# A fused attention and two-MLP kernel: GpSimd's small steps moved or dropped, plain chunks first in block two, zero-padded low halves of k

## Chip, cores and metric

The kernel runs on one core of one Trainium2 chip. The metric is the device time of one execution in microseconds; three runs of the kernel before took 1105.09, 1108.4 and 1123.04 us, median 1108.4 us.

## The reference

Causal attention over 4 batches, 8 heads, 576 tokens and 64 features with a bias from a running sum, then two blocks. Block one adds the real part of a two-dimensional FFT to its input, normalizes, and adds an MLP (512 to 2048 to 512, ReLU). Block two is the same MLP step with a gain and no FFT. The MLP weights come in double precision.

```python
scores = q @ k.T / 8                       # per batch and head
cum = cumsum(max(s, 0))
scores += min(-(cum[:, None] - cum[None, :]), 0)      # causal: -1e9 above the diagonal
scores -= max(scores); attn = exp(scores)
x = attn / (sum(attn) + 1e-9) @ v
u = x + real(fft(fft(x, axis=1), axis=2))
un = (u - mean(u)) / sqrt(var(u) + 1e-6)
x = u + max(un @ w_ch1, 0) @ w_ch2         # block one
xn = (x - mean(x)) / sqrt(var(x) + 1e-6) * g_ln
out = x + max(xn @ w2_ch1, 0) @ w2_ch2     # block two
```

## The kernel before

**Tiles.** The 576 tokens of a batch are five row tiles: A0 and A1 (tokens 1 to 256), B1 and B0 (320 to 575, kept in reversed order), and M (token 0 and 257 to 319, 64 rows, two batches share 128). A unit is one pair of heads' row tile and head; a tile sees 129, 257, 320, 448 or 576 keys. Four pairs of heads per batch make 40 units.

**Two kinds of attention.** Batches zero and one (`attn_steps32`) multiply q and k in f32; the bias of batch zero is built on TensorE out of bf16 parts of the running sum (L1033 for the key's, L1036 for the query's, L1048 for the mask), that of batch one on GpSimd. Batches two and three (`attn_steps`) split q and k into fp16 high and low halves. `prep_pair` (L647) writes them into `qk16` and one transposing DMA (L692) turns them: block 0 and 1 hold a head's q as high and low halves below each other, 2 and 3 the high half of k twice, block 4 the low half of k, head 0 in rows 0 to 63 and head 1 in rows 64 to 127. `emit_qk` (L747) takes both heads of a tile together: for each a product of 128 rows (L757), then for each one of 64 rows with k's low half (L760), then the reduction on VectorE (L762). `turn_pair` (L699) copies the reversed and the M columns of q into `qx`, partly on GpSimd.

**A unit's way.** `emit_bias` (L731, GpSimd: an addition at L735, then a triangular mask at L740), `emit_qk` or `emit_qk32`, two exponentials on ScalarE (L785, L786), the low half of the probabilities by a subtraction (L796, GpSimd or VectorE), a transposing DMA, and the product with v (`emit_pv`, L830, L843). GpSimd also clears the padding of each probability tile (L784) and adds 1e-9 to the row sums (L810).

**MLP.** The rows go in chunks of two row tiles: `emit_ln` (L316) normalizes one. VectorE takes mean and variance and a power-of-two scale p; `un` (L343, a buffer of its own) and `u16` (high and low fp16 halves) follow, a transposing DMA makes `unT` (L351), and 14 operations of one or two columns (L354 to L365, GpSimd but for L357) make the correction `f` by three Newton steps; f is multiplied into the result at the end. Block one runs `emit_g1` (L377) and `emit_g2` (L401), with the next batch's attention and FFT put between them by `Side`. Block two runs `emit_g1x` (L443) and `emit_g2x` (L471), a product scheme with seven multiplications for eight: ReLU on ScalarE (L450), four sums on GpSimd (L451 to L454), a cast on ScalarE (L456), a subtraction on VectorE (L457). Its weights are prepared by `Weights7.split` (L289), whose sums (L295) are GpSimd's too.

**Block two's chunks.** `chunk2` (L1231) loads a chunk's rows from the scratch `x2d` into eight rotating slots of `xset`: A and M tiles by the SP queue (L1242), B tiles, whose rows are reversed, by an indirect gather that GpSimd issues (L1238). L1434 sets the order.

**Order.** Every engine executes its instructions in the order in which a list scheduler put them when the kernel was built; `urgent` raises priorities and `tc.issue_after` ties the issue of some steps to others. All plain DMAs are issued by the SP queue.

**Scratch.** `fwide` and `hwide` (L66, L70) lend the attention's rotating buffers of tiles B0 and B1 to the FFT: `ftile` are score tiles, `htile` with 0 probabilities and with 1 transposed probabilities.

## Time and profile before

| | |
|---|---|
| runs | 1105.09, 1108.4, 1123.04 us; median 1108.4 |
| profiled execution | 1109.54 us, span 1107.8 us |
| busy: TensorE, VectorE, ScalarE, GpSimd | 991.9, 723.0, 567.5, 616.1 us |
| granted TensorE clock, mean | 0.952 |
| HBM read, written | 61.50 MB, 9.51 MB |

The profile is of one execution. PE is TensorE's matmul, PEld its weight load, DVE VectorE, ACT ScalarE, POOL GpSimd, SP the queue that issues DMAs. In a timeline a row may stand for several instructions of one kind (xN): its first number is the start of the first, its second the time to the end of the last. A matmul's end is modelled, so successive matmuls overlap in it; how long one holds the array is read from one start to the next. An engine's wait is put down to what ended last before it.

### The profile page before, as it was taken

How to read it: one execution, taken by the hardware profiler on the slowest of the kernel's cores; microseconds unless marked ns; L12 is line 12 of the kernel's file. 1: busy time of each engine (PE TensorE's matmuls, PEld its weight loads, DVE VectorE, ACT ScalarE, POOL GpSimd, SP SyncE). 2: the span in 40 equal slices, each digit the busy share in tenths (PEclk: the TensorE clock that was granted, in tenths of full speed). 3: DMA queues.
4: the chain of work that ended last, by engine and by line, in shares of the span. 5: the costliest groups of instructions: out<-in, count | busy, mean ns of one | idle time of the engine just before them, and what ended most of it. 6: DMA issues, size and time to landing. Idle time of an engine off the chain costs nothing.

```text
span 1107.8 us, 23630 instructions
## 1 busy us (share of the span) xinstructions
PE 991.9 (90%) x8729; PEld 745.6 (67%) x8729; DVE 723.0 (65%) x1733; ACT 567.5 (51%) x1278; POOL 616.1 (56%) x1317
## 2 busy tenths in 40 slices
...
GB/s 197 258 193 247 234 139 139 140 137 113 124 135 197 181 161 2 66 183 159 179 43 147 54 248 286 19 49 39 57 22 39 58 21 50 47 39 21 20 10 30
DMA packets 286035, 124.19 MB, mean 112 GB/s; under 512 B 267616, under 2 KB 267872, under 8 KB 285920
## 3 DMA queue, kind: packets, MB, share of 16 engines
...
q14 instruction: 47, 0.39, 0.1%
HBM read 61.50 MB, written 9.51 MB: 64 GB/s over the span
## 4 chain that ended last, share of the span: by engine, by line
PE 40%; DVE 6%; POOL 4%; DMA 2%; issue 1%; ACT 0%; SPq 0%; POOLq 0%; DVEq 0%; ACTq 0%
PE acc L471 13%; PE g L443 7%; PE g1x L443 7%; PE g L401 6%; PE g L377 5%; DMA wbbig<-in_moe_w_ch_dram 1%; POOL wbsums L295 1%; DVE wbbig L156 1%; DVE wbbig L153 1%; DVE wb L156 1%; DVE wb L153 1%; PE pv L830 1%; DVE wbbig L150 0%; PE y L1153 0%; DVE h L384 0%
## 5 line engine op out<-in xcount | busy, mean ns | idle before, releaser
L377 PE MATMUL g<-unT,wa 128*128 128x256 f16 (+1 forms) x1920 | 221.6, 267 | 3.8 <-DMA unT<-u 2.6
L401 PE MATMUL g<-wa,h 128*128 128x512 f16 x864 | 211.9, 384 | 6.0 <-DVE h L384 3.4
L377 PEld LDWEIGHTS <-wa 128*128 128x128 f16 x1920 | 173.5, 100 | 45.2 <-issue 5.9
L471 PE MATMUL acc<-wbbig,wa 128*128 128x256 f16 x1512 | 181.6, 275 | 10.7 <-ACT wa L456 6.9
L457 DVE TENSOR_TENSOR wa<-wa,wa 128x896 f16<-128x896 f32 x72 | 81.1, 1126 | 161.2 <-ACT wa L456 161.0
L443 PEld LDWEIGHTS <-wb 128*128 128x128 f16 x1728 | 169.1, 98 | 20.3
L471 PEld LDWEIGHTS <-wa 128*128 128x128 f16 x1512 | 148.7, 99 | 31.4 <-ACT wa L456 7.4
L401 PEld LDWEIGHTS <-h 128*128 128x128 f16 x864 | 81.8, 99 | 87.8 <-DVE h L384 7.4
L456 ACT CAST wa<-wa 128x896 f16<-128x896 f32 x72 | 67.4, 938 | 129.8 <-POOL wa L454 129.8
L785 ACT ACTIVATE p<-sc,mn 128x576 f16<-128x576 f32 (+4 forms) x160 | 89.7, 576 | 64.6 <-DVE mn L762 21.8
L796 POOL TENSOR_TENSOR p<-sc,p 128x129 f16<-128x129 f32 (+4 forms) x104 | 92.1, 888 | 43.1 <-ACT sc L786 38.0
L453 POOL TENSOR_TENSOR wa<-wa 128x128 f32<-128x128 f32 x72 | 48.8, 678 | 102.8 <-ACT wa L450 102.6
L443 PE MATMUL g1x<-unT,wb 128*128 128x256 f16 x864 | 101.8, 273 | 0.0
L443 PE MATMUL g<-unT,wb 128*128 128x256 f16 x864 | 100.9, 273 | 0.0
L830 PE MATMUL pv<-v,pT 128*128 128x64 f16 x1632 | 69.4, 199 | 32.1 <-DMA pT<-p 12.2
L830 PEld LDWEIGHTS <-pT 128*128 128x128 f16 x1632 | 63.6, 102 | 47.0 <-issue 24.6
L786 ACT ACTIVATE sc<-sc,mn 128x576 f32<-128x576 f32 (+4 forms) x160 | 91.7, 574 | 1.4
L735 POOL TENSOR_TENSOR sc<-cumb,ncqs 128x320 f32<-128x320 f32 (+4 forms) x80 | 68.0, 860 | 21.6 <-DVE cumb L645 11.0
L383 ACT ACTIVATE h<-g 128x512 f16<-128x512 f32 (+1 forms) x80 | 43.5, 544 | 68.9 <-PE g L377 68.4
L784 POOL MEMSET p<- 128x128 f16 (+1 forms) x160 | 36.4, 248 | 75.5 <-DMA pT<-p 43.0
L1043 PE MATMUL s<-qkT 128*128 128x288 f32 (+4 forms) x192 | 69.8, 460 | 4.7 <-DVE total L84 2.2
L384 DVE SCALAR_TENSOR_TENSOR h<-g,h 128x512 f16<-128x512 f32 (+1 forms) x80 | 50.2, 628 | 30.0 <-ACT h L383 29.8
...
## 6 DMA issues: line engine op xcount, KB each, us to landing
...
```

The costliest lines, as they stand in the source:

```text
L377: nc.tensor.matmul(out=ps[:, c * i:c * i + c], lhsT=ch.w.w1(lw, kk, m + i), rhs=ch.unT[:, 4 * lx + kk, 0:c], start=(n == 0), stop=(n == 23),)
L401: nc.tensor.matmul(out=ch.ps[j], lhsT=h[:, lh, c:c + 128], rhs=ch.w.w2(lw, m + i), start=(m + i + n == 0), stop=(m + i == MB - 1 and n == 2),)
L443: nc.tensor.matmul(out=ps, lhsT=ch.w.w1(lw, kk, m + 8 * half), rhs=ch.unT[:, 4 * lx + kk, :], start=(n == 0), stop=(n == 11),)
L456: nc.scalar.copy(out=h[:, 0], in_=r[:, 0:7])
L457: nc.vector.tensor_tensor(out=h[:, 1], in0=r[:, 0:7], in1=h[:, 0], op=ALU.subtract)
L471: nc.tensor.matmul(out=acc[key], lhsT=h[:, lh, ia], rhs=b[:, ib, lw], start=(m == 0 and i == 0 and not second), stop=(m == 7 and i == 2 an ...
L735: nc.gpsimd.tensor_tensor(out=u.f[:, 0:n], in0=P.cumb[u.h][:, 0:n], in1=P.ncq[:, t, u.h:u.h + 1].to_broadcast([128, n]), op=ALU.add)
L785: nc.scalar.activation(out=u.w[:, 0:n], in_=u.f[:, 0:n], func=AF.Exp, bias=mn, scale=-1.0)
L786: nc.scalar.activation(out=u.f[:, 0:n], in_=u.f[:, 0:n], func=AF.Exp, bias=mn, scale=-1.0, accum_out=u.rs[:, h:h + 1])
L796: eng.tensor_tensor(out=u.w[:, w:w + n], in0=u.f[:, 0:n], in1=u.w[:, 0:n], op=ALU.subtract)
L830: nc.tensor.matmul(out=ps[:, c], lhsT=pT[:, lp * nb + kb, :], rhs=P.v[:, kb, lv, c], start=(n == 0), stop=(n == 3 * nb - 1),)
L1043: nc.tensor.matmul(out=ps[:, b - a:e - a], lhsT=P.qT[:, o:o + 128], rhs=kt[:, b - k0:e - k0], start=not pe, stop=not pe or (not masked and ...
```

## The change

- **Bias.** `emit_bias` loses its addition (L735): the running sum's value at the query's own position, constant in a row, drops out of the softmax. The mask reads the key's sums directly and over the full width. The sums are taken relative to their middle value. On TensorE the query's part (L1036) goes, and with it the tables that fed it and the transposes at the start (L605).
- **Correction of the normalization.** p is now a first estimate of the reciprocal root, and f a polynomial of the fifth degree on VectorE; the multiplication by `c2` moves to VectorE too. GpSimd has no part in it.
- **Small steps.** The 1e-9 goes to ScalarE (`tiny`); the probability tiles of A0, A1 and M are cleared once and stay; `turn_pair` needs only its VectorE copy, since q is loaded in the order of the row tiles (`load_q`).
- **Scores.** `qk16` gets a sixth block: k's low half of head 0 and of head 1 stand in blocks of their own whose other 64 rows are zero, so the second product uses all 128 rows. Heads are no longer taken two at a time. The transposing DMA moves 30 blocks in place of 25.
- **Buffers.** `un` takes turns with the FFT's scratch during block one; that scratch is now the score and transposed-probability buffers of tile B0.
- **Block two.** Three chunks of A tiles and the M chunk come first.

```diff
     def fwide(name):
         turn["f"] += 1
-        return ftile(name, (B1, B0)[turn["f"] % 2], turn["f"] // 2 % 2)
+        if turn["f"] % 2:
+            return ftile(name, B0, turn["f"] // 2 % 2)
+        return htile(name, B0, turn["f"] // 2 % 2, 1).bitcast(F32)
...
-            un = mpool.tile([128, 512], F32, tag="un", name="un", bufs=1)
+            un = un_tile[0]()[:, 0:512]
...
-        nc.gpsimd.tensor_tensor(out=v, in0=va, in1=p, op=ALU.mult)
-        nc.gpsimd.tensor_tensor(out=v, in0=v, in1=p, op=ALU.mult)
...
-        for _ in range(3):
-            t = va
-            nc.gpsimd.tensor_tensor(out=t, in0=v, in1=y, op=ALU.mult)
-            nc.gpsimd.tensor_tensor(out=t, in0=t, in1=y, op=ALU.mult)
-            nc.gpsimd.tensor_scalar(out=t, in0=t, scalar1=-0.5, scalar2=1.5, op0=ALU.mult, op1=ALU.add)
-            nc.gpsimd.tensor_tensor(out=y, in0=y, in1=t, op=ALU.mult)
-        ch.f = y
+        nc.vector.tensor_tensor(out=d, in0=p, in1=p, op=ALU.mult)
+        nc.vector.tensor_tensor(out=d, in0=d, in1=va, op=ALU.mult)
+        nc.vector.tensor_scalar(out=d, in0=d, scalar1=1.0, scalar2=None, op0=ALU.subtract)
+        f = small.tile([128, 2], F32, tag="f", name="f", bufs=3)[:, 0:n]
+        nc.vector.tensor_scalar(out=f, in0=d, scalar1=RSQRT[0], scalar2=None, op0=ALU.mult)
+        for c in RSQRT[1:]:
+            nc.vector.scalar_tensor_tensor(out=f, in0=f, scalar=c, in1=d, op0=ALU.add, op1=ALU.mult)
+        ch.f = f
...
-    qk16 = att.tile([128, 5, 5, 128], F16, name="qk16")
+    qk16 = att.tile([128, 6, 5, 128], F16, name="qk16")
...
             nc.vector.scalar_tensor_tensor(
-                out=qk16[:, 4, :, 64 * h:64 * h + 64], in0=raw[:, 1, :, h, :], scalar=sc[:, 1:2],
+                out=qk16[:, 4 + h, :, 64 * h:64 * h + 64], in0=raw[:, 1, :, h, :], scalar=sc[:, 1:2],
...
-        nc.gpsimd.tensor_tensor(
-            out=u.f[:, 0:n], in0=P.cumb[u.h][:, 0:n], in1=P.ncq[:, t, u.h:u.h + 1].to_broadcast([128, n]), op=ALU.add
-        )
...
         nc.gpsimd.affine_select(
-            out=u.f[:, a:n], in_=u.f[:, a:n], pattern=[[-1, n - a]], compare_op=ALU.is_ge, fill=MASKED, base=base,
+            out=u.f[:, 0:n], in_=P.cumb[u.h][:, 0:n], pattern=[[-1, n]], compare_op=ALU.is_ge, fill=MASKED, base=base,
...
-            pss = [ps_s.tile([128, 512], F32, tag="s", name="s")[:, 0:z - a] for _ in us]
-            for u, ps, qT in zip(us, pss, qTs):
+            for u, mn, qT in zip(us, mns, qTs):
+                ps = ps_s.tile([128, 512], F32, tag="s", name="s")[:, 0:z - a]
                 nc.tensor.matmul(out=ps, lhsT=qT, rhs=kT[:, 2 + u.h, a:z], start=True, stop=False)
-            for u, ps, qT in zip(us, pss, qTs):
-                r = slice(64 * u.h, 64 * u.h + 64)
-                nc.tensor.matmul(out=ps, lhsT=qT[r], rhs=kT[r, 4, a:z], start=False, stop=True)
-            for u, ps, mn in zip(us, pss, mns):
+                nc.tensor.matmul(out=ps, lhsT=qT, rhs=kT[:, 4 + u.h, a:z], start=False, stop=True)
...
-        if u.h == 1:
-            nc.gpsimd.tensor_scalar(out=u.rs, in0=u.rs, scalar1=1e-9, scalar2=None, op0=ALU.add)
+        if h == 1:
+            nc.scalar.activation(out=u.rs, in_=u.rs, func=AF.Identity, bias=tiny, scale=1.0)
...
-        chunks = [chunk2(wb, kk) for kk in KEYS[:7] + KEYS[8:] + KEYS[7:8]]
+        chunks = [chunk2(wb, kk) for kk in KEYS[0:5:2] + KEYS[8:] + KEYS[1:6:2] + KEYS[6:8]]
```

What the new order of instructions looks like at three places follows. The first is TensorE in the scores of batches two and three. Before, with L757 for the full products and L760 for those of 64 rows:

```order
L830 MATMUL pv<-v_4534,pT 128x64
L757 LDWEIGHTS qx
L757 MATMUL s<-qkT_104,qx 128x288
L757 LDWEIGHTS qkT_104
L757 MATMUL s<-qkT_104 128x257
L760 LDWEIGHTS qkT_104
L760 MATMUL s<-qkT_104 128x257
L760 LDWEIGHTS qx
L760 MATMUL s<-qkT_104,qx 128x288
L830 LDWEIGHTS pT
```

Now, with L756 for the high and L757 for the padded low half:

```order
L756 LDWEIGHTS qx
L756 MATMUL s<-qkT_105,qx 128x288
L757 LDWEIGHTS qx
L757 MATMUL s<-qkT_105,qx 128x288
L756 LDWEIGHTS qx
L756 MATMUL s<-qkT_105,qx 128x448
L757 LDWEIGHTS qx
L757 MATMUL s<-qkT_105,qx 128x448
```

High and low products of one unit now follow each other; two units are no longer woven into each other.

The second place is GpSimd where block two begins. Before: L295 are sums for the weights, L453, L451, L452 and L454 the sums of the hidden rows (`wa_188` and `wa_187` are the two scratch buffers), L354 and L355 steps of the normalization's correction, L1238 the gathers:

```order
L295 TENSOR_TENSOR wbsums<-wbbig 128x256 x2
L295 TENSOR_TENSOR wbsums<-wbbig,wbsums 128x256
L1238 DMA xset_107<-x2d,rev 128x512
L1238 DMA xset_108<-x2d,rev 128x512 x2
L1238 DMA xset_107<-x2d,rev 128x512
L453 TENSOR_TENSOR wa_188<-wa_188 128x128
L453 TENSOR_TENSOR wa_187<-wa_187 128x128
L295 TENSOR_TENSOR wbsums<-wbbig,wbsums 128x256
L451 TENSOR_TENSOR wa_187<-wa_187 128x128
L451 TENSOR_TENSOR wa_188<-wa_188 128x128
```

Now L304 are the weights' sums and L463, L461, L462 and L464 those of the hidden rows:

```order
L304 TENSOR_TENSOR wbsums<-wbbig 128x256 x2
L304 TENSOR_TENSOR wbsums<-wbbig,wbsums 128x256
L463 TENSOR_TENSOR wa_171<-wa_171 128x128
L463 TENSOR_TENSOR wa_172<-wa_172 128x128
L304 TENSOR_TENSOR wbsums<-wbbig,wbsums 128x256
L461 TENSOR_TENSOR wa_171<-wa_171 128x128
L461 TENSOR_TENSOR wa_172<-wa_172 128x128
L462 TENSOR_TENSOR wa_171<-wa_171 128x128
```

The four gathers between the weights' sums and the hidden rows' are gone; the eight of the new program stand in pairs further down, the first one some 40 rows later.

The third place is VectorE in block one, at the normalization of the second chunk beside the attention of batch one (L343 before, L351 now, writes `un`; in brackets the engines and queues that an instruction waits for). Before:

```order
L357 TENSOR_SCALAR y<-va 128x2 [waits Pool_49]
L350 TENSOR_TENSOR u_1961<-un,u_1961 128x512 [waits DVE_49,Activation_49]
L1049 ISA sc,mn<-s,sc 128x257 [waits PE_49]
L1049 ISA mn 128x1
L97 TENSOR_SCALAR wasc<-wasc 128x1 [waits DVE_49]
L796 TENSOR_TENSOR p_2130<-sc,p_2130 128x576 [waits Activation_49]
L985 TENSOR_SCALAR qkT_105<-tp 128x256 [waits Activation_49]
L343 TENSOR_SCALAR un<-xset_107,mv,va 128x512 [waits DVE_49]
```

Now:

```order
L1023 ISA sc,mn<-s,sc 128x257 [waits PE_49]
L1023 ISA mn 128x1
L368 SCALAR_TENSOR_TENSOR f<-f,va 128x2 [waits DVE_49]
L204 SCALAR_TENSOR_TENSOR wa_170<-wa_171,wasc,wa_170 128x512 [waits Activation_49]
L351 TENSOR_SCALAR un<-xset_108,mv,va 128x512 [waits DMAHW4_49,PE_49]
L368 SCALAR_TENSOR_TENSOR f<-f,va 128x2 [waits DVE_49]
L204 SCALAR_TENSOR_TENSOR wa_171<-wa_172,wasc,wa_171 128x512 [waits Activation_49]
L1023 ISA sc,mn<-s,sc 128x257 [waits PE_49]
```

`un` waited for VectorE's own last use of its buffer; it now waits for TensorE and a DMA, the last users of the attention's buffer that it takes. The steps of `f` (L368) stand between.

## Rows read from the trace of the kernel before

**Rows 1.** Stretches: us, PE, PEld, DVE, ACT, POOL busy, PEclk, DMA share, GB/s.

```profile
0.00:165.00 165.00, 101.49 (x835) 71.26 (x835) 139.53 (x370) 107.75 (x280) 87.29 (x166) 0.82 0.87 212
165.00:285.00 120.00, 109.34 (x983) 79.07 (x983) 81.92 (x241) 82.08 (x196) 89.26 (x199) 0.93 0.69 136
285.00:550.00 265.00, 243.53 (x2158) 153.78 (x2156) 202.12 (x582) 159.03 (x385) 177.21 (x424) 0.96 0.70 136
550.00:735.00 185.00, 180.40 (x1536) 125.47 (x1535) 128.49 (x266) 78.69 (x170) 52.21 (x97) 1.00 0.42 125
735.00:800.00 65.00, 54.34 (x452) 44.89 (x451) 44.63 (x70) 27.81 (x47) 55.53 (x98) 0.92 0.20 49
800.00:1108.00 308.00, 302.75 (x2774) 271.11 (x2771) 126.36 (x208) 112.18 (x202) 154.59 (x337) 1.00 0.14 35
```

**Rows 2.** Waits of PE: us in total, times, longest us.

```profile
PE s L757 <- DVE mn L762: 7.6, 10, 1.7
...
PE g L377 <- DMA unT<-u: 2.6, 1, 2.6
```

**Rows 3.** Timeline of PE where block two begins: start, us, what.

```profile
743.87 2.78 PE L443 MATMUL g1x<-unT,wb 128*128 128x256 f16 x24
746.49 2.78 PE L443 MATMUL g<-unT,wb 128*128 128x256 f16 x24
754.83 1.89 PE L471 MATMUL acc<-wbbig,wa 128*128 128x256 f16 x8 [5.57 <-ACT wa L456]
757.58 4.62 PE L471 MATMUL acc<-wbbig,wa 128*128 128x256 f16 x21 [0.86 <-DVE wa L457]
```

**Rows 4.** Timeline of PE at two places of the fp16 scores.

```profile
357.63 0.41 PE L757 MATMUL s<-qkT,qx 128*128 128x288 f16 x2
357.97 0.29 PE L760 MATMUL s<-qkT,qx 64*128 64x288 f16 x2
...
389.37 0.27 PE L757 MATMUL s<-qkT 128*128 128x257 f16 x1
389.58 0.28 PE L760 MATMUL s<-qkT 64*128 64x257 f16 x1
389.79 0.82 PE L401 MATMUL g<-wa,h 128*128 128x512 f16 x3
```

**Rows 5.** Stretch 285 to 550, L760 alone: PE and PEld busy, clock, DMA.

```profile
285.00:550.00 265.00, 23.33 (x96) 7.26 (x96) 0.96 0.70 136
```

**Rows 6.** Groups of instructions: count | busy us, mean ns | idle before.

```profile
L735 POOL TENSOR_TENSOR sc<-cumb,ncqs 128x320 f32<-128x320 f32 (+4 forms) x80 | 68.0, 860 | 21.6 <-DVE cumb L645 11.0 <-DVE p L796 5.5 <-DVE fs L1116 1.4
L740 POOL TENSOR_SCALAR_AFFINE_SELECT sc<-sc 128x128 f32<-128x128 f32 (+1 forms) x120 | 41.3, 350 | 1.8
...
L338 DVE SCALAR_TENSOR_TENSOR va<-mv,va 128x2 f32<-128x2 f32 (+1 forms) x19 | 3.6, 188 | 0.3
...
L1129 ACT COPY eo<-xe 128x2 f32<-128x2 f32 x8 | 1.5, 193 | 14.8 <-DVE xe L1124 11.5 <-DVE eo L1131 3.3
```

**Rows 7.** Stretches after TensorE's stop at 749, columns as in the first rows.

```profile
754.80:762.00 7.20, 6.30 (x29) 4.19 (x30) 6.28 (x12) 3.85 (x7) 7.20 (x12) 0.50 0.39 73
762.00:800.00 38.00, 33.77 (x301) 28.77 (x299) 25.06 (x33) 15.90 (x28) 32.68 (x63) 1.00 0.09 20
```

**Rows 8.** Timeline of POOL where block two begins.

```profile
743.24 1.18 POOL L1238 DMA_INDIRECT xset<-x2d,rev  x1 [0.18 <-issue]
...
748.22 0.87 POOL L453 TENSOR_TENSOR wa<-wa 128x128 f32<-128x128 f32 x2
```

**Rows 9.** Groups of POOL from 735 to 800 us.

```profile
L362 POOL TENSOR_TENSOR va<-va,y 128x2 f32<-128x2 f32 x6 | 3.4, 572 | 0.0
L363 POOL TENSOR_TENSOR va<-va,y 128x2 f32<-128x2 f32 x6 | 3.2, 546 | 0.0
```

**Rows 10.** Groups of DVE, one step of the weights, block one's and block two's.

```profile
L150 DVE TENSOR_SCALAR wa<-wa 128x512 int32<-128x512 int32 x21 | 14.0, 670 | 0.5 <-DMA wa<-in_moe_w_ch_dram 0.5
...
L150 DVE TENSOR_SCALAR wbbig<-wbbig 128x512 int32<-128x512 int32 x16 | 6.5, 419 | 0.8 <-DMA wbbig<-in_moe_w_ch_dram 0.8
```

148 lines of the change are left out of this document (61 added, 87 removed).

## Prediction

> **What bounds the kernel now.** I read the stretches first, then who waits, then the timeline at two places. Cut by the work that runs, the 1107.8 us fall into six stretches [rows 1]. TensorE (PE) is busy 101 of the first 165 us and 54 of the 65 us from 735 on; in the other four it is busy 91 to 98%. In the first 165 us VectorE (DVE) is busy 139.5 us, turning the loaded weights into f32, and the DMA engines 87%: there neither TensorE nor GpSimd (POOL) sets the pace. From 285 to 550 (fp16 attention of batches two and three inside the first MLP block) TensorE is busy 243.5 of 265 us; its largest wait for scores is 7.6 us in all [rows 2]. From 800 on block two streams with TensorE at 302.8 of 308 us: nothing there can be won but by fewer matmuls, and the change removes none of those.
>
> So gains are to be had where TensorE's own time gets shorter in a full stretch (285 to 550), and where it starves (735 to 800, the first 165 us).
>
> **Part one, the score products.** Before, each score tile is a product of full rows (L757) and one of the low half of k that uses 64 rows (L760). The timeline shows what the mix costs. In block two 24 matmuls of 256 columns take from 743.87 to 746.49 [rows 3], 0.109 us each, and that is also about what 257 columns should take at 389.37. But the 257-column L757 holds the array 0.21 us before the L760 starts, and the L760 0.21 us before the next full product [rows 4]: about 0.10 us lost at each side, 0.20 us per trip to 64 rows and back. The 96 products of L760 lie in this stretch [rows 5]. Counted through the timeline, 19 of them directly follow the other head's (the pair at 357.97 shares 0.29 us, [rows 4]), so there are 77 trips: 77 x 0.20 = 15.4 us. With k's low halves padded to 128 rows there is no trip, but the 19 pairs run one after the other; a second full product of 288 columns adds 0.41 - 0.29 = 0.12 us (the two at 357.63), 19 x 0.12 = 2.3 us. Net 13 us less TensorE time; bounds -6 (the trips cost nothing, see the rivals) and 15.
>
> The Trainium skill, page "TensorEngine Tiling (Array Packing)", section Theoretical Speedup, speaks against this part: with a contraction of 64 or less, row tiling gives up to twice the speed. Its section Key Properties adds that changing the mode drains the engine; the trace has both, the shared 0.29 us and the 0.10 us per side, and the trips outnumber the pairs four to one. By the first rule alone the part would cost time; that is a rival below.
>
> How much of the 13 us arrives? DVE is busy 202 of 265 us in the stretch and POOL 177, so both have room, though not in every part of it. POOL loses the additions of L735 (80 x 0.86 = 68 us with those of the batches two and three [rows 6]), and its masks then read the full width, unseen in the trace: at least the 0.35 us that 128 columns take (L740, [rows 6]), at most the 1.21 us of both steps together, so never more than now. DVE gets the correction of each normalized chunk (about 7 instructions more at 0.19 us [rows 6], 1.3 us a chunk, 19 chunks), ACT 80 additions of two columns at about 0.19 us, 15 us in 550; both hide beside TensorE, and where DVE is full they cost their own 1 to 2 us a batch. SP issues three loads of q more for each of eight pairs, and the transposing DMA moves 30 blocks for 25; the DMA engines are 70% busy [rows 1] and the loads come a pair ahead, so I charge nothing; without that cover a pair's first scores come later by a fifth of one transfer. I take 11 of the 13 us (bounds -6 and 17, the upper with some of the 7.6 us of waits for scores gone, since a pair of heads no longer holds two PSUM buffers at once).
>
> **Part two, the start of block two.** TensorE stands still 5.57 us until 754.83, waiting for the cast of the second step's products; then 0.86 us [rows 3]. Backwards: the cast waits for POOL's four sums, and these begin at 748.22, right behind four indirect gathers that start at 743.24 [rows 8]: 5.0 us of POOL. In the changed order the first chunks are loaded by the SP queue, and no gather stands there any more. After the idle time the granted clock is 0.50 from 754.8 to 762 [rows 7], the 1.2 GHz level: 21 matmuls from 757.58 take 4.62 us [rows 3], 0.22 each; these and the 8 before them pay 0.11 us extra, 3.2 us. The small normalization steps on POOL (L362 and L363 alone 6.6 us of these 65 [rows 9]) go to DVE, which is busy 45 of 65. Sum: 5.57 + 0.86 + 3.2 = 9.6 us, plus about half of the 4.2 us that TensorE still waits between 762 and 800 (33.8 busy of 38 [rows 7]). I take 11 us; bounds 4 (the sums then wait for the weight preparation still queued on POOL, and the clock falls all the same) and 14. Late next would be the second block's weight sums (L295) on the same engine. The eight gathers come back later, one pair per chunk among sums; before, two pairs already did so while TensorE was busy 302.8 of 308 us [rows 1], so I charge 0, at most 1 us for each of the four pairs.
>
> **Part three, the first 285 us.** 48 products of the query's own cumulative sum (L1036) go, and the split parts of k become one. TensorE idles there, so this is worth little. What counts is DVE: a weight step that takes 0.42 us while POOL is nearly idle takes 0.67 us here [rows 10]; over the thirty weights of this stretch that is 30 x 0.25 = 7.5 us. POOL is relieved of memsets, of the 1e-9 additions and of a part of the bias, by my estimate a quarter of its 87 us [rows 1], so a quarter of 7.5: 2 us. From 165 to 285 TensorE idles 120 - 109.3 = 10.7 us [rows 1]; DVE no longer waits for POOL's 1e-9 additions there, and a quarter of the idle time, 2.5 us, goes. Bounds for each -1 (a few added DVE steps) and 5 to 7.5. The Trainium skill, page "SBUF — State Buffer", section SBUF: two separate sides, has a rule that would give more: some DVE instructions and GpSimd share a port pair, which one holds for its whole instruction. By it the 0.25 us above is POOL's doing, and work taken off POOL speeds DVE everywhere; that too is a rival.
>
> **Sum.** 11 + 11 + 2 + 2.5 = 26.5 us. The profiled execution took 1109.54 us (span 1107.8 and 1.7 around it), so 1083.0; it lies 1.1 us above the median of the runs, 1108.4. In terms of the median: 1082 us. Two per cent, about what a measurement of this kernel tells from no change, is 22 us: 1086.
>
> **Rivals.**
> DVE becomes the bound of the attention. For it: DVE is busy 85% where the weights are converted and 76% in the stretch of part one, and there are thicker and thinner parts in it; and it gets some 7 instructions more a chunk. TensorE's 13 us then turn into idle time: part one gives 2, part three 1.5; 1108.4 - 14.5 = 1094. Against it: TensorE is the fuller engine by 41 us in the stretch.
>
> Slower: the normalization's scratch `un` has no buffer of its own any more in block one; it takes turns with the score and the transposed-probability buffers of tile B0. In the changed program such an instruction waits for TensorE and a transposing DMA, and on DVE the score reductions and h stand behind it. If a chunk's transposed input then comes late, TensorE stands before the chunk. Today that happens once, 2.6 us [rows 2]. Six chunks are normalized beside attention; at the 5.6 us of the longest stop in these rows [rows 3] that is 34 us, 7 more than the gains: 1116. From 4.4 us each the gains are gone.
>
> More than forecast: POOL's relief speeds DVE wholly. The first stretch gives 7.5 us in place of 2, the second 5 in place of 2.5, part one its upper bound 17 in place of 11: 14 us more, 1068. For it: the 0.67 against 0.42 us of [rows 10]. Against: POOL keeps three quarters of its work in the first stretch.
>
> The tiling rule: the low products at double speed and no price for the change of mode. Then part one costs half of the 48 pairs, 48 x 0.12 = 5.8 us, in place of giving 11: 1108.4 - 26.5 + 16.8 = 1099. The 0.21 us of [rows 4] speak against it.
>
> **How the numbers follow.** Forecast (1074 to 1090) 0.48; more 0.17; DVE-bound 0.19; tiling rule 0.05; scratch 0.11. Faster by over 2%: 0.17 and 0.40 of the forecast's 0.48, 0.57. Slower by over 2% (above 1130) is the worse half of the scratch case, 0.05. The rest, 0.38, is within 2%. The range 1066 to 1104 leaves out the scratch case and some of the far end.
>
> **What would show it.** Right: in the successor of 285 to 550 no 0.10 us gaps around the low products and a stretch about 11 us shorter; no idle time of over 1 us and no clock of 0.50 in block two's first 60 us; the gathers single, among sums. Wrong: DVE above 90% in the attention with TensorE's waits for scores larger than 7.6 us; waits of L377 for unT above 2.6 us; a stretch from 735 that is still 65 us long for the same products.

## The result and the profile after

| | before | changed |
|---|---|---|
| runs | 1109.18 us median (1105.09 to 1123.04) | 1096.06 us median (1095.33 to 1097.66) |
| ratio, 95% interval | | 0.9889, 0.9859 to 0.9919 |
| span of the profiled execution | 1107.8 us | 1093.6 us |
| busy: TensorE, VectorE, ScalarE, GpSimd | 991.9, 723.0, 567.5, 616.1 us | 967.2, 720.1, 580.1, 415.3 us |
| granted TensorE clock, mean | 0.952 | 0.95 |

The change gives 13 us, 1.1%, where 26.5 were forecast. To see where, I cut both traces at the same products: the first transform product of batch one (the FFT, L1153 before, L1126 after), that of batch three, and the first product with block two's weights (L443, L453).

| stretch | before | changed | forecast for it | measured |
|---|---|---|---|---|
| A: start to batch one's transform | 270.6 us | 257.5 us | -4.5 us (part three) | -13.1 us |
| B: from there to batch three's transform (fp16 attention of batches two and three) | 295.0 | 297.7 | -11 (part one) | +2.7 |
| C: rest of block one | 165.6 | 168.5 | 0 | +2.9 |
| D: block two | 376.6 | 369.8 | -11 (part two) | -6.8 |

The four add up to 14.3 us, the difference of the two spans but for rounding. The direction is right and the places are wrong: what was to be the smallest gain is nearly the whole of it, and the stretch of part one is no shorter.

The borders are the same, the work between them not quite, since block one's chunks are woven into the attention. B of the changed kernel holds 36 more of their first products (L387, 912 for 876) and 4 more of the second (L411, 418 for 414), C holds 37 and 12 fewer, and A's chunk work 8 more of the second. At 0.11 us for 256 columns and 0.22 for 512, B has taken about 5 us of TensorE work over and C has lost about 7. If that counted in full, B would be some 2 us shorter than before for equal work (an estimate; the runs below say that it counts for less), and C, where TensorE was busy 160.9 of 165.5 us before, has lost more than its 2.9 us. Of the versions below, most agree with the changed kernel in this to ten products; runs 8, 9, 10, 13 and 17 have 14 to 16 of the first and 6 to 10 of the second fewer in B, about 3 us, nearly all of it handed to C.

Windows over parts of these stretches follow. First the kernel before (columns as in [rows 1]): of A the piece from batch zero's transform to the first chunk product, then the chunk work beside batch one; all of B, all of C, and the first 59 us of D.

```profile
134.00:176.00 42.00, 27.31 (x173) 18.81 (x174) 39.08 (x111) 25.15 (x67) 28.55 (x65) 0.74 0.66 150
176.00:270.60 94.60, 88.30 (x848) 64.49 (x848) 60.07 (x182) 65.23 (x161) 74.41 (x158) 0.95 0.70 138
270.60:565.50 294.90, 273.43 (x2513) 175.71 (x2514) 222.48 (x627) 169.13 (x407) 187.74 (x442) 0.97 0.69 135
565.50:731.00 165.50, 160.90 (x1257) 110.36 (x1254) 117.36 (x247) 74.17 (x160) 46.62 (x89) 1.00 0.41 126
731.00:790.00 59.00, 49.88 (x409) 40.65 (x408) 39.35 (x59) 26.28 (x42) 50.13 (x90) 0.91 0.21 50
```

Then the changed kernel between the same borders:

```profile
132.50:169.40 36.90, 26.96 (x171) 17.48 (x169) 34.33 (x116) 22.56 (x57) 13.28 (x27) 0.69 0.61 152
169.40:257.50 88.10, 85.75 (x824) 61.57 (x824) 61.86 (x187) 70.66 (x187) 45.50 (x80) 0.99 0.82 153
257.50:555.20 297.70, 261.61 (x2565) 182.87 (x2562) 205.61 (x651) 176.54 (x447) 98.18 (x184) 0.97 0.73 137
555.20:723.70 168.50, 158.50 (x1208) 107.53 (x1205) 129.54 (x298) 74.96 (x159) 24.58 (x29) 0.99 0.42 132
723.70:782.70 59.00, 53.92 (x472) 45.55 (x471) 41.49 (x64) 27.76 (x47) 41.38 (x62) 1.00 0.13 33
```

In the third row of each, B, TensorE is busy 273.4 us before and 261.6 after: 11.8 us less, and that with the chunk products taken over. But the stretch is 2.8 us longer, so TensorE's idle time grew from 21.5 to 36.1 us. A's 13.1 us fall into 1.5 up to batch zero's transform (134.0 to 132.5), 5.1 in the first row and 6.5 in the second (94.6 to 88.1). In the first row VectorE is busy nearly throughout in both kernels, 39.1 of 42.0 and 34.3 of 36.9 us. In the last, TensorE does 472 matmuls in 59 us for 409, and the clock is 1.00 for 0.91.

What TensorE waits for in B, changed kernel (us in total, times, longest):

```profile
PE s L756 <- DVE mn L758: 16.8, 11, 8.8
PE pv L826 <- DMA pT<-p: 7.8, 4, 3.4
PE total L91 <- ACT qk L663: 4.1, 1, 4.1
PE s L756 <- DMA qkT<-qk: 2.8, 2, 2.0
```

The first answers to [rows 2], where it was 7.6 us in 10 waits; here one wait alone takes 8.8 us. GpSimd's groups on the page of the changed kernel (name, count, then busy us and mean ns, idle before):

```profile
L739 POOL TENSOR_SCALAR_AFFINE_SELECT sc<-cumb 128x129 f32<-128x129 f32 (+4 forms) x120 | 67.4, 573 | 109.7 <-DVE p L794 40.6
L775 POOL MEMSET p<- 128x128 f16 x64 | 13.0, 204 | 112.5 <-DMA pT<-p 80.3
```

The full-width masks take 67.4 us where addition and mask took 68.0 + 41.3 [rows 6]: 0.57 us each, inside the bounds that the prediction set (0.35 and 1.21). L775 are the clears of tiles B0 and B1, which stay.

### The profile page after: what moved, and what is told of

The parts are those of the page before. It is cut to its first block, busy times and chain, and to the rows that moved or that the text cites. A ratio compares the mean times of both kernels' runs of the same rounds, so it can differ in the third digit from the quotient of the medians.

```text
span 1093.6 us, 23078 instructions
## 1 busy us (share of the span) xinstructions
PE 967.2 (88%) x8644; PEld 740.8 (68%) x8644; DVE 720.1 (66%) x1848; ACT 580.1 (53%) x1350; POOL 415.3 (38%) x717
## 3 DMA queue, kind: packets, MB, share of 16 engines
q8 instruction: 68, 1.11, 0.4%
## 4 chain that ended last, share of the span: by engine, by line
PE 38%; DVE 10%; POOL 3%; DMA 2%; ACT 1%; issue 1%; SPq 1%; ACTq 0%
PE acc L481 13%; PE g1x L453 7%; PE g L453 7%; PE g L387 4%; PE g L411 4%; POOL wbsums L304 2%; DVE wbbig L313 1%; DVE wbbig L165 1%; DMA wbbig<-in_moe_w_ch_dram 1%; DVE wbbig L162 1%; PE pv L826 1%; DVE h L394 1%; DVE wb L162 1%; DVE wb L165 1%; SPq L798 1%
## 5 line engine op out<-in xcount | busy, mean ns | idle before, releaser
L387 PE MATMUL g<-unT,wa 128*128 128x256 f16 (+1 forms) x1920 | 219.4, 265 | 1.4 <-DVE h L394 0.8
L411 PE MATMUL g<-wa,h 128*128 128x512 f16 x864 | 207.4, 382 | 9.2 <-DVE h L394 5.1
L387 PEld LDWEIGHTS <-wa 128*128 128x128 f16 x1920 | 173.9, 99 | 39.7 <-issue 3.0
L481 PE MATMUL acc<-wbbig,wa 128*128 128x256 f16 x1512 | 178.5, 273 | 6.6 <-DVE wa L467 5.3
L453 PEld LDWEIGHTS <-wb 128*128 128x128 f16 x1728 | 169.1, 98 | 20.2
L411 PEld LDWEIGHTS <-h 128*128 128x128 f16 x864 | 82.9, 99 | 92.5 <-DVE h L394 8.6
L466 ACT CAST wa<-wa 128x896 f16<-128x896 f32 x72 | 67.4, 938 | 117.3 <-POOL wa L464 117.3
L794 POOL TENSOR_TENSOR p<-sc,p 128x129 f16<-128x129 f32 (+4 forms) x104 | 94.7, 917 | 82.6 <-ACT sc L782 74.8
L781 ACT ACTIVATE p<-sc,mn 128x576 f16<-128x576 f32 (+4 forms) x160 | 90.2, 576 | 58.6 <-DVE mn L1023 16.4
L826 PE MATMUL pv<-v,pT 128*128 128x64 f16 x1632 | 72.8, 202 | 43.4 <-DMA pT<-p 24.0
L826 PEld LDWEIGHTS <-pT 128*128 128x128 f16 x1632 | 66.9, 104 | 62.3 <-DMA pT<-p 31.5
L739 POOL TENSOR_SCALAR_AFFINE_SELECT sc<-cumb 128x129 f32<-128x129 f32 (+4 forms) x120 | 67.4, 573 | 109.7 <-DVE p L794 40.6
L453 PE MATMUL g1x<-unT,wb 128*128 128x256 f16 x864 | 101.5, 273 | 0.0
L453 PE MATMUL g<-unT,wb 128*128 128x256 f16 x864 | 100.9, 273 | 0.0
L463 POOL TENSOR_TENSOR wa<-wa 128x128 f32<-128x128 f32 x72 | 46.2, 642 | 121.2 <-ACT wa L460 121.2
L1018 PE MATMUL s<-qkT 128*128 128x288 f32 (+4 forms) x192 | 74.1, 487 | 3.1 <-DVE wasc L106 1.4
L394 DVE SCALAR_TENSOR_TENSOR h<-g,h 128x512 f16<-128x512 f32 (+1 forms) x80 | 50.6, 633 | 38.0 <-ACT h L393 37.6
L393 ACT ACTIVATE h<-g 128x512 f16<-128x512 f32 (+1 forms) x80 | 43.5, 544 | 59.8 <-PE g L387 59.3
L775 POOL MEMSET p<- 128x128 f16 x64 | 13.0, 204 | 112.5 <-DMA pT<-p 80.3
## 6 DMA issues: line engine op xcount, KB each, us to landing
x2d<-o SPq DMA_DIRECT2D x18, 256.0 KB
out_dram<-wa SPq DMA_DIRECT2D x16, 256.0 KB
```

Source lines behind the costliest of these rows:

```text
L387: nc.tensor.matmul(out=ps[:, c * i:c * i + c], lhsT=ch.w.w1(lw, kk, m + i), rhs=ch.unT[:, 4 * lx + kk, 0:c], start=(n == 0), stop=(n == 23),)
L411: nc.tensor.matmul(out=ch.ps[j], lhsT=h[:, lh, c:c + 128], rhs=ch.w.w2(lw, m + i), start=(m + i + n == 0), stop=(m + i == MB - 1 and n == 2),)
L453: nc.tensor.matmul(out=ps, lhsT=ch.w.w1(lw, kk, m + 8 * half), rhs=ch.unT[:, 4 * lx + kk, :], start=(n == 0), stop=(n == 11),)
L466: nc.scalar.copy(out=h[:, 0], in_=r[:, 0:7])
L481: nc.tensor.matmul(out=acc[key], lhsT=h[:, lh, ia], rhs=b[:, ib, lw], start=(m == 0 and i == 0 and not second), stop=(m == 7 and i == 2 an ...
L739: nc.gpsimd.affine_select(out=u.f[:, 0:n], in_=P.cumb[u.h][:, 0:n], pattern=[[-1, n]], compare_op=ALU.is_ge, fill=MASKED, base=base, chann ...
```

## The experiments

Every run is the changed kernel with the edit named, but for one that edits the kernel before. The intervals are about 0.35% each way, 4 us: smaller differences are not told apart by the times, though a stretch of the trace may tell them. A to D are of one profiled execution each. The two profiles of the changed kernel differ by 1.2 us in A and under 1 us elsewhere. The list scheduler orders anew after each edit, so an edit moves more than its own instructions.

| run | median us | ratio to before, 95% interval | A | B | C | D |
|---|---|---|---|---|---|---|
| before | | | 270.6 | 295.0 | 165.6 | 376.6 |
| changed | 1096.1 | 0.9889 (0.9859 to 0.9919) | 257.5 | 297.7 | 168.5 | 369.8 |
| changed, again | 1093.4 | 0.9888 (0.9851 to 0.9924) | 256.3 | 298.4 | 168.5 | 369.9 |
| 1 chunk order back | 1094.5 | 0.9898 (0.9863 to 0.9933) | 256.3 | 296.4 | 161.4 | 375.8 |
| 2 low products on 64 rows | 1100.6 | 0.9927 (0.9895 to 0.9958) | 258.9 | 302.1 | 168.2 | 369.8 |
| 3 as 2, 25 blocks | 1094.6 | 0.9898 (0.9868 to 0.9928) | 256.8 | 296.9 | 169.3 | 369.1 |
| 4 zeros set on the chip, 25 blocks | 1091.7 | 0.9871 (0.9837 to 0.9905) | 256.2 | 294.8 | 169.1 | 369.3 |
| 5 less transposed | 1090.2 | 0.9861 (0.9826 to 0.9896) | 260.8 | 292.6 | 168.6 | 369.4 |
| 6 heads together | 1090.0 | 0.9867 (0.9832 to 0.9902) | 258.1 | 289.7 | 170.5 | 369.3 |
| 7 part one undone | 1092.8 | 0.9855 (0.9801 to 0.9910) | 256.0 | 295.6 | 169.3 | 369.7 |
| 8 GpSimd's small steps back | 1116.9 | 1.0112 (1.0070 to 1.0153) | 280.2 | 299.6 | 164.7 | 370.8 |
| 9 the same, addition later | 1111.1 | 1.0021 (1.0000 to 1.0042) | 269.7 | 304.7 | 165.5 | 371.2 |
| 10 correction back | 1092.4 | 0.9849 (0.9813 to 0.9885) | 259.3 | 295.5 | 165.3 | 371.3 |
| 11 zeroing back | 1104.1 | 0.9959 (0.9928 to 0.9990) | 266.3 | 296.9 | 168.3 | 369.0 |
| 12 1e-9 back | 1108.4 | 1.0004 (0.9978 to 1.0030) | 263.7 | 304.7 | 168.7 | 369.3 |
| 13 bias addition back | 1102.4 | 0.9965 (0.9945 to 0.9985) | 264.7 | 297.0 | 168.4 | 369.0 |
| 14 before, with 1e-9 and zeroing moved | 1111.9 | 1.0037 (1.0005 to 1.0069) | 270.9 | 293.9 | 166.2 | 376.6 |
| 15 runs 4 and 6 together | 1090.7 | 0.9831 (0.9792 to 0.9870) | 257.0 | 293.7 | 169.8 | 369.0 |
| 16 as 15, order back | 1091.5 | 0.9849 (0.9813 to 0.9884) | 257.0 | 293.3 | 161.0 | 375.3 |
| 17 as 15, correction back | 1093.2 | 0.9885 (0.9857 to 0.9913) | 258.1 | 295.6 | 166.9 | 370.9 |

The changed kernel was run again beside runs 5, 6 and 8, as a yardstick:

> The changed kernel itself, beside the next ones on the same chip: 1093 to 1098 us by every theory; it is what they are compared with.

### Block two's chunk order

```diff
-chunks = [chunk2(wb, kk) for kk in KEYS[0:5:2] + KEYS[8:] + KEYS[1:6:2] + KEYS[6:8]]
+chunks = [chunk2(wb, kk) for kk in KEYS[:7] + KEYS[8:] + KEYS[7:8]]
```

> The changed kernel with only block two's chunk order put back (gathered chunk at its old place). Theory 'order': the gathers ahead of the first sums cost what the prediction gave them, part two; the two traces show block two's first 59 us with 5.1 us of TensorE idle time in place of 9.1 and no half clock, so about 7 us are lost again: 1103 us, TensorE standing over 4 us at the block's start behind the cast, granted clock 0.50 after it. Rival 'relief': the start of block two got faster since GpSimd has less to do; then the order is worth under 2 us: 1096 to 1098 us.

Neither theory holds whole: the time is near that of 'relief', but the stop and the slow clock come back as 'order' says. TensorE's timeline of this run, at block two's start:

```profile
738.03 6.04 PE L481 MATMUL acc<-wbbig,wa 128*128 128x256 f16 x29 [5.76 <-ACT wa L466]
...
754.79 2.74 PE L481 MATMUL acc<-wbbig,wa 128*128 128x256 f16 x21 [1.56 <-ACT wa L466]
```

and its windows of the end of block one and the start of block two:

```profile
678.70:714.10 35.40, 35.25 (x242) 23.45 (x241) 23.72 (x40) 24.44 (x46) 18.77 (x20) 1.00 0.02 9
714.10:773.10 59.00, 50.95 (x420) 41.49 (x419) 43.12 (x76) 26.13 (x42) 46.31 (x61) 0.94 0.19 50
```

29 matmuls take 6.04 us behind the 5.76 us stop, 0.21 us each, near the 0.22 of [rows 3], and the granted clock is 0.54 from 738 to 744. Yet the time is the changed kernel's. In the table D loses 6.0 us, and C, in which no chunk of block two is computed, gains 7.1. With plain chunks first, the second chunk of block two is there early: its normalization (statistics to u16) runs on VectorE from 665 to 691 us, while block one's last chunk is on TensorE; in run 1 it runs from 730 to 744, behind the gathers. The changed kernel's VectorE, ScalarE, GpSimd and TensorE there:

```profile
684.90 1.11 DVE L364 TENSOR_SCALAR va<-va 128x2 f32<-128x2 f32 x1
685.93 0.68 DVE L165 SCALAR_TENSOR_TENSOR wbbig<-wbbig 128x512 int32<-128x512 int32 x1
686.53 0.68 DVE L358 TENSOR_TENSOR u<-un,u 128x512 f16<-128x512 f32 x1
687.14 1.11 DVE L366 TENSOR_SCALAR f<-va 128x2 f32<-128x2 f32 x1
688.16 0.68 DVE L394 SCALAR_TENSOR_TENSOR h<-g,h 128x512 f16<-128x512 f32 x1
```

```profile
683.82 1.50 ACT L355 ACTIVATE u<-xset,va 128x512 f16<-128x512 f32 x2
685.24 0.57 ACT L393 ACTIVATE h<-g 128x512 f16<-128x512 f32 x1
```

```profile
687.00 1.22 POOL L201 TENSOR_TENSOR wb<-wb,wb 128x512 f16<-128x512 f32 x1 [1.01 <-ACT wb L200]
```

```profile
685.86 1.04 PE L411 MATMUL g<-wa,h 128*128 128x512 f16 x4 [1.71 <-ACT h L393]
688.90 2.64 PE L411 MATMUL g<-wa,h 128*128 128x512 f16 x8 [2.00 <-DVE h L394]
```

TensorE waits 1.71 and 2.00 us for h, and h stands behind the normalization's steps: on ScalarE the high half (L393) behind L355, on VectorE the low half (L394) behind L364, L358 and L366. Two of these take 1.11 us for two columns, the second beside GpSimd's 1.22 us step. With the old order the same 35.4 us hold 0.2 us of idle time. So the new order, in the changed kernel, moves idle time from one side of the border to the other: about 7 us won in block two, about 7 us lost before it. Run 16 says the same on other ground (D +6.3, C -8.8 against run 15):

> As the run with heads together and zeros set on the chip, and block two's chunks in the order of before the change. Theory 'moved wait' (the new order only moves TensorE's idle time from block two's start to block one's last chunk, where the earlier normalization stands ahead of h on VectorE): within 2 us of that run, 1084 to 1089 us. Theory 'order': 5 to 7 us more than that run, 1090 to 1095 us.

It came out 0.8 us above run 15, so 'moved wait', though both lie above the absolute numbers expected.

### Part one: the score products

Run 2 puts the 64-row product back and leaves the blocks:

```diff
-nc.tensor.matmul(out=ps, lhsT=qT, rhs=kT[:, 4 + u.h, a:z], start=False, stop=True)
+r = slice(64 * u.h, 64 * u.h + 64)
+nc.tensor.matmul(out=ps, lhsT=qT[r], rhs=kT[r, 4 + u.h, a:z], start=False, stop=True)
```

> The changed kernel with the low products back on 64 rows of k, all else as it is (the padded blocks are still made, transposed and moved). Theory 'DMA': in the fp16 attention the DMA engines set the pace (their share is 0.97 to 1.05 in the ten-microsecond windows from 327 to 407 us and from 467 us on), TensorE waits anyway; 96 trips of 0.20 us, 19 us more TensorE time, then mostly go into what was idle (36 us): 1096 to 1102 us. Theory 'TensorE' (that of the prediction): the stretch is as long as TensorE's work, so 13 to 19 us come back: 1109 to 1115 us.

4.2 us by the ratios, where 'TensorE' wanted 13 to 19. The price of the trip itself is as the prediction read it. First the changed kernel (its second profile), a pair of 129 columns, then this run:

```profile
331.02 0.22 PE L756 MATMUL s<-qkT 128*128 128x129 f16 x1
331.07 0.22 PE L757 MATMUL s<-qkT 128*128 128x129 f16 x1
331.13 2.32 PE L411 MATMUL g<-wa,h 128*128 128x512 f16 x10
```

```profile
333.93 0.22 PE L756 MATMUL s<-qkT 128*128 128x129 f16 x1
334.08 0.23 PE L758 MATMUL s<-qkT 64*128 64x129 f16 x1
334.24 1.04 PE L411 MATMUL g<-wa,h 128*128 128x512 f16 x4
```

From start to start 0.05 and 0.06 us, against 0.15 and 0.16: 0.20 us per trip, at 129 columns as at 257. Added up from start to start, the 192 score products of a run hold TensorE 38.0 us before, 27.3 after, 43.7 in run 2 (96 single trips). The Trainium skill's page "TensorEngine Tiling (Array Packing)", section Theoretical Speedup, says that a contraction of 64 can go up to twice as fast by row tiling. Single 64-row products among full ones were slower here, 0.16 against 0.06 us. The Trainium skill's section Key Properties on the same page says that a change of the tiling mode drains TensorE. The 0.10 us lost at each side agree with it. But 16.4 us more TensorE time made B only 3.7 to 4.4 us longer; the rest went into time in which TensorE had been idle.

Runs 3 and 4 ask whether the DMA engines are what TensorE waits for. Run 3 puts both low halves into one block as before:

```diff
-out=qk16[:, 4 + h, :, 64 * h:64 * h + 64], ...
+out=qk16[:, 4, :, 64 * h:64 * h + 64], ...
-out=P.qkT.rearrange(...), in_=qk16.rearrange(...)
+out=P.qkT[:, 0:5].rearrange(...), in_=qk16[:, 0:5].rearrange(...)
```

> As the run with 64-row low products, and k's two low halves share one block again, so that a pair's transposing DMA moves 25 blocks for 30. Theory 'DMA': 40 blocks less; 4105 packets fewer by the kernel before, of 25 ns on 16 engines, 6 to 8 us, and up to 14 by the busy share: 6 to 14 us less than the run with 30 blocks, 1086 to 1094 us. Theory 'TensorE': the same as that run, 1109 to 1115 us. Rival 'emission' (the waits come from the heads being taken one at a time): the same as that run within 3 us.

Run 4 takes that transfer with the full products, and sets the zeros afterwards in `turn_pair`:

```diff
+nc.gpsimd.memset(P.qkT[0:64, 5, :], 0.0)
+nc.vector.tensor_copy(out=P.qkT[64:128, 5, :], in_=P.qkT[64:128, 4, :])
+nc.gpsimd.memset(P.qkT[64:128, 4, :], 0.0)
```

> The changed kernel with full 128-row low products, but 25 blocks in the transposing DMA: the zeros are set on the chip, by one copy of 64 x 640 on VectorE and two memsets on GpSimd per pair. Theory 'DMA': 6 to 10 us less than the changed kernel, 1086 to 1090 us, with smaller waits for transposed probabilities and scores. Theories 'TensorE' and 'emission': no gain, 0 to 4 us more for the added steps, 1096 to 1100 us.

Run 3 is 6 us below run 2 by the medians and 5 us shorter in B, at the edge of what 'DMA' expected; run 4 is 1.9 us below the changed kernel by the ratios and 3 to 4 us in B, less than the 6 to 10 expected. With the heads taken singly the sixth block costs something near 4 us, but the intervals overlap. Run 5 was the sharper test:

```diff
-out=u.pT[:, 0:2 * w].rearrange(...), in_=u.w[:, 0:2 * w]
+out=u.pT[:, 0:w].rearrange(...), in_=u.w[:, 0:w]
-lhsT=pT[:, lp * nb + kb, :]
+lhsT=pT[:, (0 if t in (B0, B1) else lp) * nb + kb, :]
```

> The changed kernel, but the transposing DMA of the probabilities of tiles B0 and B1 moves the high half alone, and the products with the low half read the high one again (low halves of these probabilities are left out of the output; TensorE's, VectorE's, ScalarE's and GpSimd's work is the same). That takes 18 of a pair's 98 blocks off the DMA engines, in all 16 pairs. Theory 'DMA': with about 0.2 us a block, 29 us of DMA time in the fp16 attention; TensorE idles 36 us there, so 12 to 25 us less: 1071 to 1084 us, waits for transposed probabilities and for scores down by more than half. Theories 'TensorE' and 'emission': under 4 us less, 1092 to 1098 us.

18 of the 98 blocks that a pair of the fp16 attention moves are gone, and 3 us with them (5 to 6 in B, of which 3 to 5 are given back in A). TensorE's waits for transposed probabilities in B fell from 7.8 to 3.4 us, but those for `qkT` grew from 2.8 to 5.4, and 14.2 us of waits for VectorE stayed. 'DMA' as the one bound falls.

Run 6 takes both heads together again:

```diff
-emit_qk(us[i:i + 1])
+if us[i].h == 0:
+    emit_qk(us[i:i + 2])
```

> The changed kernel with both heads of a score tile emitted together again in the fp16 attention (as before; the products stay 128 rows). Theory 'emission' (one head at a time makes TensorE wait for the reductions of the scores): 5 to 10 us less, 1086 to 1091 us, and the waits of the score products for VectorE fall from 17 to under 8 us. Theory 'DMA': within 4 us of the changed kernel, 1092 to 1100 us.

1090.0 us is within what 'emission' expected, though its interval overlaps the changed kernel's; the trace is clearer, B is 8 us shorter. The waits of the score products for VectorE fell from 16.8 to 6.9 us, and the one of 8.8 us is gone. (Heads together do not always do this: in runs 7 and 15, which have them too, these waits are 12.1 and 11.8 us, the longest 7.0 and 5.0.) The wait of 8.8 us is worth reading in the changed kernel. TensorE and VectorE first, where batch three's attention starts anew behind the transform:

```profile
457.53 0.40 PE L756 MATMUL s<-qkT,qx 128*128 128x288 f16 x1 [8.77 <-DVE mn L758]
```

```profile
448.94 0.93 DVE L655 TENSOR_SCALAR cumb<-cumb,scs 128x576 f32<-128x576 f32 x2
...
456.95 0.52 DVE L758 CUSTOM_DVE_ANT_0 sc<-s,sc,scs 128x288 f32<-128x288 f32 x1 [1.39 <-POOL sc L739]
```

and GpSimd's own timeline:

```profile
443.01 1.17 POOL L794 TENSOR_TENSOR p<-sc,p 128x129 f16<-128x129 f32 x2 [2.62 <-ACT sc L782]
449.58 0.47 POOL L739 TENSOR_SCALAR_AFFINE_SELECT sc<-cumb 128x129 f32<-128x129 f32 x1 [5.40 <-DVE cumb L655]
450.02 1.82 POOL L794 TENSOR_TENSOR p<-sc,p 128x257 f16<-128x257 f32 x1
...
455.44 1.48 POOL L739 TENSOR_SCALAR_AFFINE_SELECT sc<-cumb 128x320 f32<-128x320 f32 x3
```

The reduction at 456.95 waits for a mask. GpSimd stood 5.40 us before the next pair's mask, since VectorE had scaled that pair's sums only at 448.94; then low halves and masks had to be made up in order, until 457. No engine is full there: the queues are long, and the wait goes round from VectorE to GpSimd to VectorE to TensorE.

Last, part one undone wholly (heads together, full products first, then the 64-row ones, 25 blocks):

> The changed kernel with part one undone wholly: 64-row low products in the order of before (both heads together, full ones first), 25 blocks in the transposing DMA. Theory of the prediction: part one is worth 11 us, so 1104 to 1109 us. Theory 'hidden' (TensorE's shorter products go into waits that end at VectorE, GpSimd and the DMA): within 4 us of the changed kernel, 1090 to 1098 us; and within 5 us of the run with full products, heads together and 25 blocks.

1092.8 us: 'hidden'. The window of B in this run:

```profile
256.00:551.60 295.60, 274.81 (x2565) 178.23 (x2561) 209.63 (x652) 176.66 (x448) 101.81 (x184) 0.97 0.68 133
```

TensorE is busy 274.8 us, 13.2 more than in the changed kernel, and the stretch is 2 us shorter. Part one, as it was made, is worth nothing here.

Heads and blocks differ between these two as well, so this does not yet price TensorE's time by itself. Run 15 (below) does: like run 7 it takes the heads together and moves 25 blocks, but its low products are full ones, each behind its own high one, and the zeros are set on the chip. B there:

```profile
257.00:550.70 293.70, 262.80 (x2565) 183.15 (x2562) 212.03 (x660) 177.98 (x447) 107.77 (x198) 0.97 0.71 134
```

TensorE is busy 12.0 us less than in run 7, and B is 1.9 us shorter. Run 4 against run 3 says the same (14.2 less, 2.1 shorter), and so does the changed kernel against run 2 (14.6 less, 4.4 shorter). So of 12 to 15 us that the padding takes off TensorE, 2 to 4 arrive, and the heads taken singly and the sixth block together take as much back: undone, as in run 15, they make B 4 to 5 us shorter than in the changed kernel. In these three pairs the chunk products in B are the same in number.

### GpSimd's small steps

Run 8 puts back the correction's steps (14 small instructions a chunk), the 1e-9 and the zeroing of every probability tile:

```diff
-nc.vector.scalar_tensor_tensor(out=f, in0=f, scalar=c, in1=d, op0=ALU.add, op1=ALU.mult)
+nc.gpsimd.tensor_scalar(out=f, in0=f, scalar1=c, scalar2=None, op0=ALU.add)
+nc.gpsimd.tensor_tensor(out=f, in0=f, in1=d, op=ALU.mult)
...
-nc.scalar.activation(out=u.rs, in_=u.rs, func=AF.Identity, bias=tiny, scale=1.0)
+nc.gpsimd.tensor_scalar(out=u.rs, in0=u.rs, scalar1=1e-9, scalar2=None, op0=ALU.add)
...
+if w > n:
+    nc.gpsimd.memset(u.w[:, 0:2 * w].rearrange("p (r w) -> p r w", r=2)[:, :, n:w], 0.0)
```

> The changed kernel with GpSimd's small operations put back: the steps of the normalization's correction, the addition of 1e-9, and the zeroing of the padding of each probability tile. Theory 'relief' (VectorE runs faster where GpSimd is idle: weight steps 670 ns before and 580 after; and nothing stands in GpSimd's queue): most of the 13 us that the changed kernel has gained by 257 us are lost, 7 to 12 us: 1103 to 1108 us, and the first product of the first block's chunks moves from 169 back to 173 to 176 us. Rival 'fewer products' (the first 257 us are shorter since 48 products and the turning of k's sums are gone): under 3 us more, 1096 to 1099 us.

23.4 us by the medians, twice what 'relief' expected, and slower than before. I had put the addition right behind the exponentials, ahead of the low half of the head before. Run 9 moves that one line into `emit_lo`, behind the transposing DMA:

> As the run with GpSimd's small operations put back, but the addition of 1e-9 stands where it stood before the change, behind the low half of its own head and the transposing DMA, and not behind the exponentials, ahead of the low half of the head before. Theory 'place' (that run's 23 us came from GpSimd waiting at the addition for ScalarE while the low halves stood behind it): most of the 23 us go, 1094 to 1099 us, first product of the first block near 170 us. Theory 'relief' (what counts is how long GpSimd is busy beside VectorE): at least half of it stays, 1103 to 1115 us, first product of the first block at 174 us or later.

Between the two theories, closer to 'relief': the place is worth 6 us by the medians and 10 by the ratios and in A, the steps themselves 15 to 18 us. Which of them? First the correction alone:

> The changed kernel with only the correction steps of the normalization (14 small instructions a chunk) put back on GpSimd. Theory 'relief': 14 x 0.2 to 0.5 us a chunk on GpSimd, beside which VectorE's SBUF steps run 1.3 to 3 times as long, and fewer steps on VectorE itself (8 of 0.15 to 0.4 us): the two nearly cancel, 1092 to 1098 us. Theory 'queue' (a chunk's factor is late when it stands in GpSimd's queue, and TensorE waits for it): 4 to 10 us more, 1097 to 1104 us.

No loss, rather a gain of 1 to 4 us, which the intervals do not tell from nothing: by the time these steps cost on VectorE about what they cost on GpSimd. So it is the other two. Zeroing alone, as in run 8 and nothing else:

> The changed kernel with the zeroing of the padding back for every unit, and nothing else. Theory 'addition' (the 17 us of the small operations are VectorE's wait for GpSimd's 1e-9): within 3 us of the changed kernel, 1092 to 1099 us. Theory 'zeroing' (a memset that waits for the transposing DMA of the tile before holds up GpSimd's queue): 8 us or more, 1103 to 1110 us.

The 1e-9 alone, at its old place:

> The changed kernel with the 1e-9 addition back on GpSimd at its old place, and nothing else. Theory 'addition': 8 to 17 us more, 1103 to 1112 us, VectorE waiting about 36 us in all for this addition at its reciprocals, and the stretch of batch one (169 to 256 us) near 97 us in place of 87. Theory 'zeroing': under 4 us more, 1093 to 1099 us.

Each is right about itself: 7.8 us for the zeroing and 12.8 us for the addition, by the ratios, and together (run 9, with the correction) 14.7. They don't add, which fits that both hold up the same queue. VectorE's waits for the addition over the whole program, kernel before:

```profile
DVE rs L1092 <- POOL rs L810: 20.0, 14, 2.9
...
DVE rs L909 <- POOL rs L810: 15.6, 14, 2.1
```

and the run with the addition back:

```profile
DVE rs L1066 <- POOL rs L806: 16.3, 15, 3.1
...
DVE rs L904 <- POOL rs L806: 14.7, 10, 2.3
```

35.6 and 31.0 us in 28 and 25 waits; in batch one's chunks, 176 to 270.6 us, the kernel before spent 19.1 us in 12 such waits. In the changed kernel what is left there is

```profile
DVE rs L1066 <- ACT rs L786: 2.8, 4, 1.6
```

The addition takes GpSimd 0.3 us in the mean for two columns, but it stands in the queue behind low halves of about 1 us each, and VectorE's reciprocal at the head of its own queue waits for it with everything behind.

Run 14 makes the same two edits on the kernel before, and nothing else:

> The kernel before with two edits alone: the 1e-9 addition on ScalarE, and the padding zeroed once for the tiles A0, A1 and M. Theory 'relief alone': it takes the 10 us of batch one's stretch and some in the fp16 attention, 10 to 16 us less than before, 1092 to 1098 us: all of the changed kernel's gain. Rival 'needs the rest' (GpSimd, with the bias additions still on it, is late anyway): under 5 us less, 1103 to 1108 us.

It gains nothing (3.7 us slower, interval 0.0005 to 0.0069). Batch one's chunks take 5.9 us less than before there, 88.7 for 94.6, and the stretch ahead of them, from batch zero's transform to the first chunk product, takes 8.9 us more: there VectorE is busy 43 of 51 us, and the scheduler has put more of batch one's scores into it (TensorE's work there grew from 27 to 34 us). The start up to batch zero's transform gave the other 2.7 us. Run 13 asks the other way round, with only the bias addition put back:

```diff
+nc.gpsimd.tensor_tensor(out=u.f[:, 0:n], in0=P.cumb[u.h][:, 0:n], in1=zero1.to_broadcast([128, n]), op=ALU.add)
+a, base, step = {A0: (1, 0, 1), A1: (129, 0, 1), M: (257, -1 - mo, 1), B1: (320, 127, -1), B0: (448, 127, -1)}[t]
 nc.gpsimd.affine_select(
-    out=u.f[:, 0:n], in_=P.cumb[u.h][:, 0:n], ...
+    out=u.f[:, a:n], in_=u.f[:, a:n], ...
```

> The changed kernel with one more pass of GpSimd per score tile: the cumulative sums are first copied with an addition (of a zero column), then masked in their last columns alone, as before the change; 112 additions of 0.4 to 1.6 us, about 90 us of GpSimd's time, less some 20 for the narrower masks. Theory 'GpSimd late' (any of the reliefs counts only when GpSimd, with all of them, has slack): 8 us or more, 1102 to 1110 us, most of it by 270 us. Rival 'two waits alone' (only the 1e-9 and the zeroing count, since VectorE and the transposing DMA stand next to them): under 4 us, 1093 to 1099 us.

8.4 us lost, 7 to 8 of them in A: 'GpSimd late'. Three quite different steps (0.3, 0.25 and 0.86 us long in the mean, the last in [rows 6]) each cost 8 to 13 us when put back alone. The amount of GpSimd's work does not say what a step costs: up to 565 us run 10 adds 25 us of it (212 to 238) and loses nothing, run 11 adds 24 and loses 7.8. I read it as one queue: what counts is whether it is late for the engine that waits next. For the addition the waits above show this. For the other two it is argued; what the traces show is that TensorE's waits for transposed probabilities in batch one's chunks grow from 2.3 us to 6.8 (run 11) and 6.4 (run 13). And none of runs 8 to 13 makes the piece from batch zero's transform to the first chunk product more than 2.4 us longer again, so the 5.1 us gained there have another cause, which no run shows.

### Putting the better parts together

Runs 4 and 6 in one kernel, and that with the correction back on GpSimd:

> The changed kernel with both heads emitted together and with the zeros set on the chip (25 blocks in the transposing DMA). If the two losses are different ones (waits for GpSimd's masks at a batch's start; a DMA queue that is full in the middle), they add up: 3.4 and 2 to 4 us less than the changed kernel, 1085 to 1088 us. If both only feed the same bound, no more than the better of the two: 1089 to 1092 us.

> The changed kernel with heads together, zeros set on the chip (25 blocks), and the correction steps of the normalization back on GpSimd. If the three small gains seen one by one (3.4, 2 to 4 and 1 to 4 us) add: 1083 to 1088 us; if they feed one bound: 1088 to 1092 us.

1090.7 and 1093.2 us: they don't add. In B heads together give 8.0 us with 30 blocks (run 6), but 1.1 with 25 (run 15 against run 4) and 1.3 with 64-row products (run 7 against run 3); 25 blocks give 2.9 us with the heads singly (run 4), and with the heads together B is 4.0 us longer (run 15 against run 6). So neither has a price of its own; both undone together give 4.0 us in B. Run 15 has the lowest ratio, 0.983, but its interval still overlaps the changed kernel's, so no version here is shown to beat it.

## Why the prediction went wrong

**What bounds the kernel.** "TensorE is the fuller engine by 41 us in the stretch" is true [rows 1] and was read as if TensorE set the pace there. It didn't: where runs differ by 12 to 15 us of TensorE time in B, the stretch differs by 2 to 4 us (runs 7 and 15, 3 and 4, 2 and the changed kernel). An engine busy 92% of a stretch can still be the one that waits; that its waits for scores came to only 7.6 us [rows 2] said that they were short, not that removing work would shorten the stretch.

**Part one.** The mechanism and its size held: 0.20 us per trip, 77 trips, 13 us net forecast, 10.7 us measured from start to start (38.0 to 27.3). The step that failed is "I take 11 of the 13 us": 2 to 4 arrive. And inside it stand two covers. "A pair of heads no longer holds two PSUM buffers at once" was to take waits away; they grew from 7.6 to 16.8 us, and putting the pairs back makes B 8 us shorter. And "I charge nothing" for the 30 blocks: B is 3 to 5 us shorter with 25. Both hold for the changed kernel alone; with the other cover undone, the pairs give 1 us in B, and 25 blocks do not shorten it (run 15). The bound of -6 below was there; the wrong end was picked.

**Part two.** The mechanism held at its place: TensorE stops 5.76 us with the gathers in front (run 1), and the clock stands at 1.00 in these 59 us, where it was 0.91. Its idle time there fell from 9.1 to 5.1 us; of what is left the longest stop is 2.87 us, another 1.37:

```profile
741.35 1.05 PE L481 MATMUL acc<-wbbig,wa 128*128 128x256 f16 x8 [0.48 <-ACT wa L466]
746.03 1.59 PE L481 MATMUL acc<-wbbig,wa 128*128 128x256 f16 x13 [2.87 <-DVE wa L467]
```

so 7 us for 11. The step that failed is that nothing was charged for a chunk that comes earlier: its normalization went ahead of h on VectorE and ScalarE, and block one's end gave the 7 us back (run 1). The "about half of the 4.2 us" was a guess with no row behind it.

**Part three.** Right in kind, and far too small. "2.5 us" for VectorE's waits for the 1e-9 was a quarter of TensorE's idle time; VectorE's own wait list had 19.1 us in that stretch, which the sum did not use. A was forecast at 4.5 and gave 13.1: up to the first chunk product 6.6 us where 2 were forecast, behind it 6.5 where 2.5 were. These two terms are the step that failed here, by their size. The other mechanism named there was real as well. The first step of block one's weights, VectorE, changed kernel, against 14.0 us and 670 ns in [rows 10]:

```profile
L159 DVE TENSOR_SCALAR wa<-wa 128x512 int32<-128x512 int32 x21 | 12.1, 580 | 0.3 <-DMA wa<-in_moe_w_ch_dram 0.3
```

With the nine steps that read `xset` (5.7 us before, 4.3 after) the thirty weights take 3.3 us less here, 2.2 in the second profile, for the 2 us forecast. That explains the 6.6 us only in part.

**Rivals.** DVE-bound: no; VectorE's share in B fell from 75 to 69%, though its time, 1094, came closest. What it described, TensorE's savings turning into idle time, happened, but not because VectorE was full. Scratch: no; waits of L387 for unT are 0.7 us in B, and GpSimd's masks waited once, 1.7 us, for `un` to be read. More than forecast: in A yes, in B no. Tiling rule: no, by the 0.20 us above, though its time, 1099, was 3 us off.

**What was to show it.** No gaps around the low products: seen. A shorter stretch: not seen. Idle time under 1 us at block two's start: no, 2.87 and 1.37; no clock of 0.50 there: seen. The gathers single among sums: they now come in pairs at 783, 823, 862 and 940 us, and TensorE is idle 1.5 us in all after 782.7, as little as before.

**Still open.** What does bound B. TensorE's time counts for 15 to 30% there (the three pairs of runs above), the transposing DMA alone is not it (run 5), nor are the heads alone (run 6), and the gains of runs 4 and 6 don't add. Waits in it go round between several engines, and I have no experiment that names one. Open too is what shortened the piece before the first chunk product by 5.1 us, and why run 14 gives its gain back.
